# Local and global attention with two MLPs on one core: the last twelve steps' keys and queries copied through DRAM and transposed as fp32r

## The chip, the cores and the metric

The kernel runs on one core of a Trainium2 chip. The metric is the device time of one execution in microseconds (us). TensorE is written PE (its weight loads PEld), VectorE DVE, ScalarE ACT, GpSimd POOL; SyncE (SP) issues nearly all DMA transfers.

## What is computed

Attention comes first: 4 batches, 8 heads, 512 local and 32 global rows of 64 elements. Each local row looks at the global keys and at local keys at most 32 places away; each global row looks at all. Its output (2176 rows of 512) goes through two MLPs. The core of it:

```python
s_g = scale * q_g @ concat(k_g, k_l).T ; out_g = softmax(s_g) @ concat(v_g, v_l)
s_l = concat(scale * q_l @ k_g.T, where(|i - j| <= 32, scale * q_l @ k_l.T, -1e9))
out_l = softmax(s_l) @ concat(v_g, v_l)
x = concat(out_g, out_l)                      # 2176 x 512
h = x @ w_in    # 512 x 2048 ; x = maximum(0.01 * h, h) @ w_out
h = x @ w2_in ; out = (h - tanh(h)) @ w2_out
```

The weights arrive as 64-bit floats, the attention inputs as 32-bit floats.

## The kernel before

The attention is cut into 32 steps, `pp` = 0 to 31: a step is two heads of one half (256 rows) of one batch. Two neighbouring steps share one load group `g` = `pp // 2`, so there are 16 groups, and groups 10 to 15 (steps 20 to 31) are batch 2's second half and the whole of batch 3. `load_kq(g)` issues seven transfers on SP's queue: three key tiles `kr` and two pieces of global keys through `keyed`, and two query tiles `qr`; each has three buffers. `stage(s)` is the work of a step, and its `keys` part holds, in this order, `k_prep(s + 1)`, `q_prep(s + 1)` and, for even `s`, `load_kq((s + 6) // 2)`; so group 10 is loaded in stage 14 and first used in stage 19.

`k_prep` transposes a step's three key tiles on PE against the fp32 identity `ident` (128, 96 and 128 columns, into the PSUM bank `kps`), and ACT copies the bank out to `kt`. `q_prep` does the same with two tiles of 128 columns (`qps`, `qt`). `score` multiplies the two (`sps`), and softmax, the transposes of the probabilities (`p_trans`, `ptps`) and the product with the values (`av`, tile `vr`) follow.

The matmuls of the MLPs (`h`, `y`, and `o` in the second MLP) have fp32r operands: each fp32 operand is split into a high and a low fp32r part, and three products are added. The scores, the products with the values and all transposes are fp32.

A loop over `n` walks over 160 items. Items 0 to 79 are the first MLP, each one block `f` of 128 hidden columns for one piece of tokens `c`; the pieces are 512, 512, 256, 512 and 384 columns wide. Items 80 to 159 are the second MLP. The attention's steps 0 to 9 run ahead of the loop; the later ones are spread between the matmuls of the items by the table `beside`: steps 10 to 17 beside items 0 to 7, 18 to 21 beside items 24 to 31, 22 to 29 beside items 32 to 47, and the rest beside items 48 to 58. PE's order is the program's order (`manual_schedule`). The other engines and the DMA queues are put in order by a list scheduler that runs when the program is built: an instruction goes to its engine's queue when it is ready in a simulated timeline, and among ready ones the earlier in the program goes first. `tc.issue_after(x)` ties what its block issues behind the instruction `x`, in order only, and only what lies on the same engine as `x`.

Two such anchors matter here. `last_kq[0]` is the last query transfer issued so far (on SP from group 2 on), and `anchor[0]` is the last `tensor_sub` of `mlp1_g` (on DVE, line 215). Weights come by `load_w` (`inraw`, `wraw`) and go through DRAM (`wod`, `w2id`, `w2od`) as raw words.

Of the kernel before, what the change touches and what calls it, by code (L numbers as in the profile page):

```python
# [8 lines left out]
F32 = mybir.dt.float32  # L9
F32R = mybir.dt.float32r  # L10
# [11 lines left out]
def kernel(  # L22
# [14 lines left out]
    nc = tc.nc  # L37
    B, H, SL, D = q_l.shape
    SG = q_g.shape[2]
# [5 lines left out]
    HALF = SL // 2  # L45
# [13 lines left out]
    dram = ctx.enter_context(tc.tile_pool(name="dram", bufs=1, space=bass.MemoryType.DRAM))  # L59
    psum = ctx.enter_context(tc.tile_pool(name="psum", bufs=1, space=bass.MemoryType.PSUM))  # L60

    def bank(tag, name):
        return psum.tile([128, 512], F32, tag=tag, name=name)
# [15 lines left out]
    ident = persist.tile([128, 128], F32, name="ident")  # L79
# [15 lines left out]
    def f32(t):  # L95
        return t.bitcast(F32)
# [76 lines left out]
    anchor, anchor_s = [None], [None]  # L173
    last_av = [None]
    last_exp, last_min = [None], [None]
    last_kq, last_fetch = [None], [None]
# [109 lines left out]
    att = att_ctx.enter_context(tc.tile_pool(name="att", bufs=2))  # L286
# [6 lines left out]
    def build_masks():  # L293
        make_identity(nc, ident)
        nc.gpsimd.memset(mask, 0.0)
        make_identity(nc, ident_b)
        for a in range(2):
            for j in range(2):
                w0, w1 = windows[a][j]
                if w1 - w0 < WIN:  # L300
                    nc.gpsimd.memset(mask[:, a, j, w1 - w0 :], BIG)
                lo, hi = max(w0, SG), min(w1, KC - SG)
                k0 = first_key[a] + lo - SG - (a * HALF + j * 128)
                m = mask[:, a, j, lo - w0 : hi - w0]
                for base, step in ((32 - k0, -1), (32 + k0, 1)):
                    nc.gpsimd.affine_select(
                        out=m, in_=m, compare_op=ALU.is_ge, fill=BIG,
                        base=base, pattern=[[step, hi - lo]], channel_multiplier=-step,
                    )
# [20 lines left out]

    v_t = {}

    def place_of(g):
        hv, h0 = divmod(4 * g, H)
        b, a = divmod(hv, 2)
        return b, a, slice(h0, h0 + 4)

    def keyed(dst, local, glob, b, a, hs, queues=None):
        queues = queues or [nc.sync] * 3
        for t in range(3):  # L340
            k0 = first_key[a] + 96 * t
            l, g = (slice(32, 128), slice(0, 32)) if t == 0 else (slice(0, 96), slice(96, 128))
            queues[t].dma_start(out=dst[l, t], in_=local[b, hs, k0 : k0 + 96, :].rearrange("h s d -> s h d"))
            if t != 1:
                queues[t].dma_start(out=dst[g, t], in_=glob[b, hs].rearrange("h s d -> s h d"))

    def load_kq(g):

        if g >= NU // 4:
            return  # L350
        b, a, hs = place_of(g)
        qr = att.tile([128, 2, 4, D], F32, tag="qr", name="qr", bufs=3)
        kr = att.tile([128, 3, 4, D], F32, tag="kr", name="kr", bufs=3)

        keyed(kr, k_l, k_g, b, a, hs, [nc.sync, nc.sync, nc.scalar] if g == 0 else None)
        queue = nc.scalar if g < 2 else nc.sync
        for t in range(2):
            s0 = a * HALF + t * 128
            last_kq[0] = queue.dma_start(out=qr[:, t], in_=q_l[b, hs, s0 : s0 + 128, :].rearrange("h s d -> s h d"))
        for k in range(2):  # L360
            h2 = slice(2 * k, 2 * k + 2)
            raw_t[2 * g + k] = qr[:, :, h2, :], kr[:, :, h2, :]
# [12 lines left out]

    key_tiles = [(0, 128), (128, 96), (224, 128)]

    def k_prep(pp, tag):
        kr = raw_t[pp][1]
        ps = bank(tag, "kps")  # L380
        for t, (c, n) in enumerate(key_tiles):
            nc.tensor.transpose(ps[:, c : c + n], kr[:n, t].rearrange("p h d -> p (h d)"), ident[:n, :n])  # L382
        kt = att.tile([128, KC], F32, tag="kt", name="kt", bufs=2)
        nc.scalar.activation(kt, ps[:, :KC], AF.Copy)
        k_t[pp] = kt

    def q_prep(pp, tag):
        qr = raw_t[pp][0]
        ps = bank(tag, "qps")
        for t in range(2):  # L390
            nc.tensor.transpose(  # L391
                ps[:, t * 128 : t * 128 + 128], qr[:, t].rearrange("p h d -> p (h d)"), ident
            )
        qt = att.tile([128, HALF], F32, tag="qt", name="qt", bufs=2)
        nc.scalar.activation(qt, ps[:, :HALF], AF.Copy, scale=-0.125)
        q_t[pp] = qt
# [346 lines left out]
    def stores():  # L743
        while later:
            later.pop(0)()
# [38 lines left out]
    def in_job():  # L784
        *parts, high, low = in_parts() or [lambda: None] * 2
        for part in parts:
            behind(part)
        high()
        low()
# [170 lines left out]
    if True:  # L960
# [2 lines left out]
        nc.vector.memset(tc_a1, T_A1)  # L963
        nc.vector.memset(tc_a2, T_A2)
        build_masks()
        for e in e_t:
            nc.gpsimd.memset(e[:, :, :, 192:], 0.0)
        for t in (*qgd, vg):
# [8 lines left out]
        parts, lows = [], []  # L977
        for pp in range(PRE):
# [3 lines left out]
            if pp >= 2 and pp % 2 == 0:  # L982
                lows, parts = parts[5:], in_parts()
# [54 lines left out]
        for n in range(len(items) + 8):  # L1038
            ph, c, f = items[n] if n < len(items) else (3, 0, 0)
            one = items[n - 1] if 0 < n <= len(items) else (3, 0, 0)  # L1040
            if n in (2 * NF + 4, 3 * NF):
                tags[0] = run_tags + (["y2", "y3"] if n < 3 * NF else [])
            if ph == 1:
                if n in (0, 2, 4, 6) or HF <= n < 2 * HF:
                    in_job()
                if n in (0, 2) or 4 <= n < 12:
                    in_load()
                for _ in range(job_at.get(n, 0)):
                    job()
                if n in (3 * HF + 3, 3 * HF + 5):  # L1050
                    y_part((n - 3 * HF - 3) // 2)
                if c == 4 and f == 0:
                    while gtodo:
                        gtodo.pop(0)[1]()
                    assert not raws and not jobs
                    att_ctx.close()
                    p2 = ctx.enter_context(tc.tile_pool(name="p2", bufs=1))
                    for k in range(NF - 1):
                        wo2_t.append([p2.tile([128, ND, 128], F32R, name=f"wo2{x}{k}") for x in "hl"])
                    wo2_t.append([x[1][:, :, 512:] for x in (xh, xl)])  # L1060
                    x2_load(0, 0)
                    x2_load(0, 1)
                if c == 4:
                    w2_fetched = [fetch2(w2o_dram[f], False), fetch2(w2i_dram[f], f >= 2 + ND)]
                    if 2 <= f < 2 + ND:
                        x2_split(0, f - 2)
            elif ph == 2 and order2.index(c) + 1 < 5:
                nx = order2[order2.index(c) + 1]
                if f in (2, 3):
                    x2_load(nx, f - 2)  # L1070
                if 5 <= f < 5 + ND:
                    x2_split(nx, f - 5)
            if n in fetch_at:
                fetches.extend(items1[m][2] for m in fetch_at[n])
            while fetches:
                wo_fetch(fetches.pop(0))
            ops = beside.pop(n, [])
            if ph == 2:
                mlp2_a(c, f)
            if ph == 3:  # L1080
                while p_t:
                    mlp2_split()
            steps, last = [], []
            for k in b_at.get(n, []):
                p, c1, f1 = items[k]
                if p == 1:
                    steps += mlp1_b(c1, f1)
                else:
                    last.append((c1, f1))
            if ph == 1:  # L1090
                steps = mlp1_a(c, f) + steps
            if ph == 1 and not ops and gtodo:
                ops = [gtodo.pop(0)[1]]
            K, M = len(ops), len(steps)
            at = [int((i + 0.5) * M / K) for i in range(K)]
            for m, step in enumerate(steps):
                step()
                while at and at[0] <= m:
                    at.pop(0)
                    ops.pop(0)()  # L1100
            for op in ops:
                op()
            for c1, f1 in last:
                mlp2_b(c1, f1)
            if ph == 1 and c == 4:
                for kind, t in zip(("out", "in"), w2_fetched):
                    behind(lambda: w2_place(kind, f, t))
            fix(n + 1)
            stores()
# [30 lines left out]
```

## Time and profile before

| | us |
|---|---|
| median of 3 runs | 917.92 |
| lowest, highest | 917.36, 918.85 |
| the profiled execution | 918.29 |
| its span in the trace | 916.5 |
| PE busy in the span | 898.9 (98%) |
| DVE, ACT, POOL busy | 626.5, 537.5, 36.4 |

How to read it: the trace holds one execution, 1.8 us shorter in span than its own measured time. The page lists busy time by engine, then groups of instructions, with what ended the idle time before them. The view by stretches gives each engine's busy time, the granted PE clock and the DMA engines' busy share between two times. The timeline lists instructions with their start. A record of a matmul is longer than the time it holds PE, since neighbours overlap: its pace is read from the start of one to the start of the next.

### The profile page before, as it was taken

How to read it: one execution, taken by the hardware profiler on the slowest of the kernel's cores; microseconds unless marked ns; L12 is line 12 of the kernel's file. 1: busy time of each engine (PE TensorE's matmuls, PEld its weight loads, DVE VectorE, ACT ScalarE, POOL GpSimd, SP SyncE). 2: the span in 40 equal slices, each digit the busy share in tenths (PEclk: the TensorE clock that was granted, in tenths of full speed). 3: DMA queues.
4: the chain of work that ended last, by engine and by line, in shares of the span. 5: the costliest groups of instructions: out<-in, count | busy, mean ns of one | idle time of the engine just before them, and what ended most of it. 6: DMA issues, size and time to landing. Idle time of an engine off the chain costs nothing.

```text
span 916.5 us, 15297 instructions
## 1 busy us (share of the span) xinstructions
PE 898.9 (98%) x5384; PEld 759.6 (83%) x5384; DVE 626.5 (68%) x1374; ACT 537.5 (59%) x1245; POOL 36.4 (4%) x70
## 2 busy tenths in 40 slices
PE   7989999999999999999999999999999999999998
PEld 4667778888778999888889998888888888899897
DVE  3987876766546656552233459888878888888886
ACT  5988865444655676553243566565556555655564
POOL 4400000000000000000000000000000000000022
PEclk9999999999999999999999999999999999999999
DMA  8786796678767977756546762001000100010010
GB/s 194 213 207 194 225 313 219 204 237 255 241 183 232 277 212 235 266 191 186 193 167 205 249 196 81 0 18 65 1 1 24 46 1 1 1 46 1 1 36 24
DMA packets 133917, 129.20 MB, mean 141 GB/s; under 512 B 72400, under 2 KB 96208, under 8 KB 133840
## 3 DMA queue, kind: packets, MB, share of 16 engines
q1 hardware_dynamic: 131040, 127.44, 45.4%
q10 hardware_dynamic: 2800, 0.79, 0.4%
q8 instruction: 42, 0.69, 0.3%
q14 instruction: 35, 0.29, 0.1%
HBM read 101.45 MB, written 26.74 MB: 140 GB/s over the span
## 4 chain that ended last, share of the span: by engine, by line
PE 86%; ACT 4%; DMA 4%; DVE 4%; issue 1%; POOL 0%; SPq 0%; ACTq 0%; POOLq 0%; DVEq 0%
PE h L55 38%; PE o L55 20%; PE y L55 18%; DMA wraw<-in_moe_w_out_dram 2%; PE sps L55 2%; PE ptps L483 2%; PE avps L55 2%; ACT e L453 1%; PE kps L382 1%; PE sgps L55 1%; PE gavps L55 1%; PE qps L391 1%; DMA inraw<-in_moe_w_in_dram 1%; ACT g L213 1%; DVE wt L137 0%
## 5 line engine op out<-in xcount | busy, mean ns | idle before, releaser
L55 PE MATMUL h<-xh,win 128*128 128x512 f32 (+2 forms) x1280 | 355.1, 361 | 0.6 <-ACT g L213 0.6
L55 PEld LDWEIGHTS h<-xh,win 128*128 128x128 f32 x1280 | 229.3, 188 | 33.8 <-ACT g L213 1.8
L55 PE MATMUL h<-xl,win 128*128 128x512 f32 (+2 forms) x640 | 228.9, 358 | 0.0
L215 DVE TENSOR_TENSOR gl<-g,gh 128x512 fp32r<-128x512 f32 (+2 forms) x80 | 48.8, 610 | 133.8 <-ACT gh L214 133.7
L55 PEld LDWEIGHTS h<-xl,win 128*128 128x128 f32 x640 | 120.5, 188 | 15.3
L55 PE MATMUL y<-gh,woh 128*128 128x512 f32 (+2 forms) x320 | 119.2, 373 | 0.0
L55 PE MATMUL y<-gh,wol 128*128 128x512 f32 (+2 forms) x320 | 114.4, 357 | 0.0
L55 PE MATMUL y<-gl,woh 128*128 128x512 f32 (+2 forms) x320 | 114.1, 358 | 0.0
L213 ACT ACTIVATE g<-h 128x512 f32<-128x512 f32 (+2 forms) x80 | 42.6, 533 | 109.6 <-PE h L55 109.5
L55 PE MATMUL o<-wo2l,gh 128*128 128x512 f32 x255 | 99.6, 391 | 0.0
L55 PE MATMUL o<-wo2h,gh 128*128 128x512 f32 x255 | 99.4, 390 | 0.0
L55 PE MATMUL o<-wo2h,gl 128*128 128x512 f32 x255 | 97.4, 390 | 0.0
L667 ACT ACTIVATE u<-h 128x512 f32<-128x512 f32 (+2 forms) x80 | 42.6, 533 | 90.5 <-PE h L55 82.8
L692 ACT ACTIVATE gh<-p 128x512 fp32r<-128x512 f32 (+2 forms) x80 | 45.5, 568 | 41.0 <-DVE p L676 41.0
L55 PEld LDWEIGHTS y<-gh,woh 128*128 128x128 f32 x320 | 60.2, 188 | 8.8 <-issue 1.9
L55 PEld LDWEIGHTS y<-gl,woh 128*128 128x128 f32 x320 | 60.2, 188 | 7.9
L55 PEld LDWEIGHTS y<-gh,wol 128*128 128x128 f32 x320 | 60.3, 189 | 6.4
L453 ACT ACTIVATE e<-e,st 128x224 f32<-128x224 f32 (+1 forms) x88 | 40.3, 459 | 30.0 <-DVE st L446 29.8
L673 ACT ACTIVATE u<-u,consts 128x512 f32<-128x512 f32 (+2 forms) x80 | 52.7, 659 | 6.4 <-DVE p L671 3.8
L693 DVE TENSOR_TENSOR gl<-p,gh 128x512 fp32r<-128x512 f32 (+1 forms) x64 | 41.8, 653 | 21.4 <-ACT gh L692 21.3
L55 PEld LDWEIGHTS o<-wo2h,gl 128*128 128x128 f32 x255 | 47.8, 188 | 10.1
L55 PEld LDWEIGHTS o<-wo2l,gh 128*128 128x128 f32 x255 | 47.9, 188 | 9.0
(118 smaller groups left out, 1397.0 us busy)
## 6 DMA issues: line engine op xcount, KB each, us to landing
wraw<-in_moe_w_out_dram SPq DMA_DIRECT2D x32, 512.0 KB, 4.4
woh<-wod SPq DMA_DIRECT2D x64, 256.0 KB, 3.9
wol<-wod SPq DMA_DIRECT2D x64, 256.0 KB, 3.4
inraw<-in_moe_w_in_dram SPq DMA_DIRECT2D x16, 512.0 KB, 5.7
wraw<-in_moe_w_in_dram SPq DMA_DIRECT2D x16, 512.0 KB, 4.9
vr<-in_v_l_dram SPq DMA_DIRECT2D x48, 96.0 KB, 4.0
kr<-in_k_l_dram SPq DMA_DIRECT2D x47, 96.0 KB, 3.1
vn<-in_v_l_dram SPq DMA_DIRECT2D x8, 512.0 KB, 4.6
```

The lines of the kernel that those rows point to most:

```text
L55: nc.tensor.matmul(o, lhsT, rhs, start=start, stop=stop, skip_group_check=shared)
L213: nc.scalar.activation(g[:, :N], h[:, :N], AF.Prelu, alpha=0.01)
L215: anchor[0] = nc.vector.tensor_sub(gl[:, :N], g[:, :N], f32(gh)[:, :N])
L382: nc.tensor.transpose(ps[:, c : c + n], kr[:n, t].rearrange("p h d -> p (h d)"), ident[:n, :n])
L391: nc.tensor.transpose(ps[:, t * 128 : t * 128 + 128], qr[:, t].rearrange("p h d -> p (h d)"), ident)
L453: last_exp[0] = nc.scalar.activation(e[:, h, j, s0 : s0 + n], x, AF.Exp, bias=st[:, k : k + 1], scale=-1.0, accum_out=st[:, 4 + k : 5 + k],)
L483: nc.tensor.transpose(ps[:, at : at + n], e[:n, h, j, c0 : c0 + 128], ident[:n, :n])
L667: nc.scalar.activation(u, h, AF.Square)
L673: nc.scalar.activation(u, u, AF.Square, bias=tc_a2)
L692: nc.scalar.activation(gh[:, :N], p, AF.Copy)
L693: eng["pool" if i == order2[-1] else "dve"].tensor_sub(gl[:, :N], p, f32(gh)[:, :N])
```

## The change

For groups 10 to 15 keys and queries no longer come straight from the inputs. `stage_in` copies them unchanged from the inputs into DRAM tiles of the kernel (`k_st`, `q_st`, `kg_st`), and `load_kq` reads those tiles into `kr` and `qr`, which for these groups are declared fp32r and written through an fp32 view, so that the words stay as they are. Their transposes then take an fp32r identity, `ident_r`, which DVE copies from `ident` at the start. Batch 2's five copies stand at items 1 to 3 of the loop and carry `last_kq[0]` as anchor; batch 3's five stand at items 10, 12, 14, 16 and 18 and carry `anchor[0]`. A copy of keys or queries covers four heads; of batch 2 only rows from 224 (keys) and 256 (queries) on are copied.

```diff
+    G1 = 10
+    k_st, q_st = [dram.tile([2, H, SL, D], F32, name=f"{x}_st") for x in "kq"]
+    kg_st = dram.tile([2, H, SG, D], F32, name="kg_st")
+    ident_r = att.tile([128, 128], F32R, name="ident_r", bufs=1)
+    first_st = [SL - 288, 0], [HALF, 0]
+
+    def stage_in(b, part, anchor):
+        with tc.issue_after(anchor.ins):
+            if part == 0:
+                nc.sync.dma_start(out=kg_st[b - 2], in_=k_g[b])
+                return
+            dst, src, lo = ((k_st, k_l, first_st[0][b - 2]), (q_st, q_l, first_st[1][b - 2]))[part % 2]
+            hs = slice(0, 4) if part < 3 else slice(4, 8)
+            nc.sync.dma_start(out=dst[b - 2, hs, lo:], in_=src[b, hs, lo:])
...
-        qr = att.tile([128, 2, 4, D], F32, tag="qr", name="qr", bufs=3)
-        kr = att.tile([128, 3, 4, D], F32, tag="kr", name="kr", bufs=3)
-
-        keyed(kr, k_l, k_g, b, a, hs, [nc.sync, nc.sync, nc.scalar] if g == 0 else None)
+        dt = F32 if g < G1 else F32R
+        qr = att.tile([128, 2, 4, D], dt, tag="qr", name="qr", bufs=3)
+        kr = att.tile([128, 3, 4, D], dt, tag="kr", name="kr", bufs=3)
+
+        if g < G1:
+            q_in, bq = q_l, b
+            keyed(kr, k_l, k_g, b, a, hs, [nc.sync, nc.sync, nc.scalar] if g == 0 else None)
+        else:
+            q_in, bq = q_st, b - 2
+            keyed(f32(kr), k_st, kg_st, b - 2, a, hs)
...
+    def transposed(out, x, n):
+        if x.dtype == F32R:
+            nc.tensor.transpose(out.bitcast(F32R), x, ident_r[:n, :n])
+        else:
+            nc.tensor.transpose(out, x, ident[:n, :n])
...
-            nc.tensor.transpose(ps[:, c : c + n], kr[:n, t].rearrange("p h d -> p (h d)"), ident[:n, :n])
+            transposed(ps[:, c : c + n], kr[:n, t].rearrange("p h d -> p (h d)"), n)
...
         build_masks()
+        nc.vector.tensor_copy(ident_r, ident)
...
+            if 1 <= n < 4 or 10 <= n < 20 and n % 2 == 0:
+                b, parts = (2, (0, 1, 2, 3, 4)) if n < 4 else (3, (0, 1, 2, 3, 4))
+                for k in (parts[2 * n - 2 : 2 * n] if n < 4 else parts[(n - 10) // 2 :][:1]):
+                    stage_in(b, k, last_kq[0] if n < 4 else anchor[0])
```

## Rows read from the trace of the kernel before

**Rows 1.** The page's first lines: span, and each engine's busy time.
```profile
span 916.5 us, 15297 instructions
PE 898.9 (98%) x5384; PEld 759.6 (83%) x5384; DVE 626.5 (68%) x1374; ACT 537.5 (59%) x1245; POOL 36.4 (4%) x70
```

**Rows 2.** Busy time by stretches; the last three columns are PE clock, DMA share, GB/s.
```profile
core 0: us, PE busy (x) PEld busy (x) DVE busy (x) ACT busy (x) POOL busy (x), PEclk, DMA share, GB/s
36.00:60.00 24.00, 22.16 (x240) 16.89 (x241) 21.22 (x58) 21.75 (x75) 6.35 (x8) 1.00 0.85 228
60.00:77.00 17.00, 15.07 (x151) 11.10 (x148) 11.14 (x45) 15.10 (x49) 0.15 (x1) 1.00 0.80 209
77.00:90.00 13.00, 13.00 (x86) 10.31 (x86) 10.95 (x33) 9.72 (x26) 0.30 (x1) 1.00 0.67 198
...
226.00:375.00 149.00, 148.53 (x1222) 129.49 (x1221) 84.09 (x285) 93.17 (x273) 0.91 (x6) 1.00 0.78 234
```

**Rows 3.** Timeline of PE around the transposes of step 22: start, length, instruction.
```profile
266.18 0.62 PE L55 MATMUL h<-xh,win 128*128 128x512 f32 x2
...
266.87 0.47 PE L382 MATMUL kps<-ident,kr 128*128 128x128 f32 x3
267.18 0.38 PE L391 MATMUL qps<-ident,qr 128*128 128x128 f32 x2
267.31 0.71 PE L55 MATMUL h<-xh,win 128*128 128x512 f32 x2
```

**Rows 4.** The chain that ended last, in order of time: fp32r matmuls of three widths.
```profile
146.08 2.72 PE y L55 x12
...
503.43 2.08 PE y L55 x12
...
861.03 1.43 PE h L55 x12
```

**Rows 5.** Instructions of line 534, the transposes with 32 columns: min/median/max in ns.
```profile
L534 PE MATMUL qgps<-ident,qgr x16: 220/222/311, 6.6 to 297.4; 32*128 32x32 f32 x16
```

**Rows 6.** Timeline of PE: four such transposes in a row.
```profile
100.20 0.43 PE L534 MATMUL qgps<-ident,qgr 32*128 32x32 f32 x4
```

**Rows 7.** Timeline of ACT: the copies of the queries out of PSUM, steps 21 and 27.
```profile
254.40 0.38 ACT L395 ACTIVATE qt<-qps 128x256 f32<-128x256 f32 x1
...
328.49 0.38 ACT L395 ACTIVATE qt<-qps 128x256 f32<-128x256 f32 x1
```

**Rows 8.** Timeline of PE: the scores that read them, same two steps.
```profile
255.37 0.46 PE L55 MATMUL sps<-kt,qt 64*128 64x224 f32 x2
...
328.89 0.60 PE L55 MATMUL sps<-kt,qt 64*128 64x192 f32 x4
```

**Rows 9.** Timeline of SP's queue: transfers as they are issued, 26 to 95 us.
```profile
26.72 0.51 SPq L581 DMA_DIRECT2D vn<-in_v_l_dram  x1
...
30.53 0.38 SPq L343 DMA_DIRECT2D kr<-in_k_l_dram  x1
...
50.77 0.48 SPq L345 DMA_DIRECT2D vr<-in_v_g_dram  x1
...
74.33 1.51 SPq L359 DMA_DIRECT2D qr<-in_q_l_dram  x2
...
77.04 0.38 SPq L581 DMA_DIRECT2D vn<-in_v_l_dram  x1
82.43 0.35 SPq L113 DMA_DIRECT2D wraw<-in_moe_w_out_dram  x1
...
90.61 0.31 SPq L343 DMA_DIRECT2D kr<-in_k_l_dram  x1
```

**Rows 10.** Transfers into the value tile `vr` issued from 36 to 62 us.
```profile
DMA to landing us min/median/max: 2.6/5.3/6.9
```

**Rows 11.** Timeline of PE: the product with the values of step 8.
```profile
59.18 0.94 PE L55 MATMUL avps<-pt,vr 128*64 128x128 f32 x16
```

**Rows 12.** The page's traffic in 40 slices of the span, GB/s.
```profile
GB/s 194 213 207 194 225 313 219 204 237 255 241 183 232 277 212 235 266 191 186 193 167 205 249 196 81 0 18 65 1 1 24 46 1 1 1 46 1 1 36 24
```

More of the change, by code (lines that the diff above doesn't have):

```diff
@@ L358, in load_kq @@
             s0 = a * HALF + t * 128
-            last_kq[0] = queue.dma_start(out=qr[:, t], in_=q_l[b, hs, s0 : s0 + 128, :].rearrange("h s d -> s h d"))
+            last_kq[0] = queue.dma_start(
+                out=(qr if g < G1 else f32(qr))[:, t], in_=q_in[bq, hs, s0 : s0 + 128, :].rearrange("h s d -> s h d")
+            )
         for k in range(2):
@@ L390, in q_prep @@
         for t in range(2):
-            nc.tensor.transpose(
-                ps[:, t * 128 : t * 128 + 128], qr[:, t].rearrange("p h d -> p (h d)"), ident
-            )
+            transposed(ps[:, t * 128 : t * 128 + 128], qr[:, t].rearrange("p h d -> p (h d)"), 128)
         qt = att.tile([128, HALF], F32, tag="qt", name="qt", bufs=2)
```

## Prediction, made before the changed kernel ran

> **What bounds the kernel now.** I read the page's engine line first. PE is busy for 898.9 of 916.5 us [rows 1], so PE work taken away should shorten the run unless something else is just as late. That share is an average, so I then read the view by stretches. The changed steps lie between 226 and 375 us, where PE works 148.53 of 149 us and DVE and ACT have 56 to 65 us to spare: PE alone sets the pace there. From 36 to 60 us it is different: PE 22.16, DVE 21.22 and ACT 21.75 of 24 us are all nearly full, and the DMA engines are 0.85 busy. From 77 to 90 us the DMA share is 0.67 [rows 2]. So PE time is worth its full length late, and transfers are dangerous early. The granted clock is 1.00, the 2.4 GHz level, in every stretch read, and I expect it to stay.
>
> **What the transposes cost now.** A step has five: three into kps, two into qps. In step 22 kps starts at 266.87 and the next matmul at 267.31, 0.44 us later. That matmul's pair takes 0.71 us where the pair before the transposes took 0.62, so it is held 0.09 us more: together 0.53 us for five, some 108 ns for one of 128 columns and less for the one of 96 [rows 3]. The records themselves are longer, but they overlap, so only the steps between starts count.
>
> **What one costs as fp32r.** No row shows an fp32r transpose. The nearest rows are the fp32r matmuls at three widths: twelve take 2.72 us at 512 columns, 2.08 at 384 and 1.43 at 256, or 227, 173 and 119 ns each [rows 4]. The steps of 54 ns per 128 columns lie on one line, which gives 65 ns at 128 columns. Below that there is a floor: four fp32 transposes of only 32 columns occupy 0.43 us, and with 0.22 us for a record the step is (0.43 - 0.22) / 3 = 70 ns, although each still loads 128 columns of weights [rows 5, 6]. So the low end is 65 to 70 ns. The high end is today's 108, because words of 32 bits are moved either way. Dearer is possible too: nothing in the trace excludes that so narrow an fp32r operation takes a slower path. I take 68 ns, since the fp32r rows are the nearest in operand type: five take 0.34 us, and a step saves 0.53 - 0.34 = 0.19 us.
>
> One row beside it: a transpose's record here is 220 ns and more even with 32 columns [rows 5], most of it latency. The Trainium skill ("TensorE: Matmul & The Clock Gate", Part 4: PE-mode transpose) gives about 275 ns for a bf16 transpose inside a kernel and puts most of it down to the access latency of SBUF. Read as a price for each, it says that the type does not matter and the saving is zero; that is the first rival. The steps between starts in [rows 3] are far under 275 ns, so here the latency overlaps and the rule is not the pace.
>
> **What of it reaches the end.** Twelve steps change. The transposes feed ACT's copies, and those feed the scores, so ACT could become the later one. In step 27 the copy of the queries ends at 328.49 + 0.38 = 328.87 and the scores start at 328.89: ACT is already last there, and the saving is lost. In the other eleven steps there is room; the least is in step 21, where the copy ends at 254.78 and the scores start at 255.37, 0.59 us later [rows 7, 8]. So 11 x 0.19 = 2.1 us. After the loads nothing else of the step changes: five transposes, two ACT copies, the same widths.
>
> The copy of the identity runs once on DVE at the start, which by the program has only two memsets before it and no scores to read yet; I cost it at nothing, and it would cost its length, under 1 us, if DVE's first work waited behind it. The loads of groups 10 to 15 keep their number, rows and bytes, so SP's issue time for them stays.
>
> **What the copies cost.** Ten transfers are added. Batch 2's carry 2 x 294,912 (keys) + 2 x 262,144 (queries) + 65,536 bytes, 1.18 MB; batch 3's 4 x 524,288 + 65,536, 2.16 MB. All are issued on SP's queue, about 0.5 us of issue each, 5 us over the run. Batch 2's first two are tied behind group 8's last query, the other three behind group 9's, issued from 74.33 us. SP issues nothing between 77.42 and 82.43 us, and group 10 is loaded from 90.61 us on [rows 9]. At the 198 GB/s of that stretch [rows 2] 1.18 MB take 6 us, so they land before 90 us; if late, group 10's loads wait on SP and hold back what stands behind them: the next raw weights, the stores of `wod`, the `inraw` loads. Group 10 itself isn't needed before step 20, at about 240 us. Cost nothing, up to 1 us if the cover is gone.
>
> Batch 3's copies are the open point. Their anchor is a DVE instruction and they are issued on SP; the tie holds only on one engine, so it does not hold them. They have no inputs to wait for, so the scheduler may issue them at any point at which SP's simulated queue has nothing earlier ready. That it does so shows: the `vn` transfer at 26.72 us belongs to stage 6, and it is issued before group 5's keys of stage 4, at 30.53 us [rows 9]. The copies can therefore lie anywhere from about 27 us, where `vn` shows SP first out of earlier work, to the places that the program gives them, items 10 to 18. Hidden, they cost nothing; the third part prices the bad place. Their need, group 12's load at about 228 us, is far off in any case.
>
> **Sum.** 918.29 of the profiled execution less 2.1 is 916.2. That execution is 0.37 us above the median of 917.92, so against the median: 917.92 - 2.1 = 915.8 us.
>
> **Rival 1: the transposes hardly get shorter.** For it: a transpose moves full 32-bit words in both types, and today's 108 ns are about twice what 128 columns cost in the matmuls' line (54 ns), as if each word went in two halves. If that belongs to the word and not to the identity, nothing is saved: 917.9 us. If half the difference stays (about 88 ns), 11 x 0.1 = 1.1 us are saved: 916.8. Against it: the fp32r rows run at one column per step of 0.42 ns.
>
> **Rival 2: batch 3's copies are issued early and PE waits.** From 36 to 60 us the DMA engines have 0.15 x 24 = 3.6 us free [rows 2]. 2.16 MB at that stretch's 228 GB/s take 9.5 us, so what is queued behind slips by up to 5.9 us. The values of step 8 are issued until 50.77 us, land 5.3 us later in the median, at 56.1, and are used at 59.18 [rows 9 to 11]: 3.1 us of room. PE, in its fixed order, then waits 5.9 - 3.1 = 2.8 us. I allow the same once more for a second late load of that stretch, 5.6 us; with the 2.1 saved, 921.4 us. It decides as soon as the copies stand ahead of 50 us and cost more than 3.1 us of delay; after 60 us nothing is close enough.
>
> How they spread over the DMA engines adds to it. At the best slice's 313 GB/s [rows 12] one of the 16 engines moves 19.6 GB/s. The Trainium skill ("DMA: Bandwidth & Descriptors", "Why a DMA increments its semaphore by 16 and not by 1") says that a transfer runs on the largest number of engines, up to 16, that divides its outermost dimension on both sides: a copy whose outermost dimension is four heads gets four. By that rule one batch-3 copy puts 131 KB on each of four engines, an estimated 6.7 us, and the four copies 27 us, which would cost far more than 5.6 us in that stretch. No run here shows it; contiguous copies may be cut otherwise.
>
> **Rival 3: narrow fp32r is slower.** Four times the matmul line's column cost would be 4 x 54 = 216 ns a transpose: 12 x 5 x 0.108 = 6.5 us longer, 924.4 us. Only the lack of any fp32r row under 256 columns speaks for it.
>
> **How the numbers follow.** About 0.2% (1.84 us) is what a measurement of this kernel can tell from no change: under 916.08 counts as faster, over 919.76 as slower. Forecast, shorter transposes and hidden copies, 915.3 to 916.1 us: 0.36. Rival 1, 916.1 to 918.5: 0.34. Rival 2, 919.8 to 922 and above: 0.26. Rival 3: 0.04. So faster 0.36, same 0.34, slower 0.30. The low bound is the 65 ns of [rows 4] in all twelve steps, 12 x 0.205 = 2.5 us, and 0.5 us for the measurement: 914.9. The high bound takes in rival 2 at 922.5 and leaves its far end and rival 3 out.
>
> **What the profile will show.** Right: 60 PE transposes of lines for kps and qps with starts 65 to 70 ns apart, five in about 0.34 us; the h, y and o groups unchanged; PE's busy time down by about 2 us; batch 3's copies after 60 us. Rival 1: the same steps near 108 ns. Rival 2: those copies on SP ahead of 50 us, avps or gavps waiting for vr or vg, PE busy less than 22 of 24 us between 36 and 60 us. The forecast is also wrong if the new order on ACT and DVE, which the scheduler makes afresh, moves other waits by more than 1 us.

## Result and the profile after

| | before | after |
|---|---|---|
| median, us | 918.1 (917.36 to 918.85, 6 runs) | 924.26 (921.2 to 925.21, 6 runs) |
| the profiled execution | 918.29 | 923.55 |
| its span | 916.5 | 921.8 |
| PE busy in the span | 898.9 | 901.5 |

After takes 1.006 times as long as before, with a 95% interval of 1.0047 to 1.0073. By that ratio the change made the kernel 5.5 us slower (the medians lie 6.2 us apart); the forecast was 2.1 us faster. Rival 3 gave 924.4 us, within 0.2 us of the measured time, but by chance: it wanted slower fp32r transposes, and they got shorter, as the rows below show. Rival 2 gave 921.4 us, 3 us less than measured; its kind of loss is what happened.

The span grew by 5.3 us, PE's busy time by 2.6. So PE lost time in two ways, about half each: it stood idle 2.7 us longer, and it took longer over the same 5384 operations. The page's first lines of after, which answer to [rows 1]:

```profile
span 921.8 us, 15307 instructions
PE 901.5 (98%) x5384; PEld 761.8 (83%) x5384; DVE 627.7 (68%) x1375; ACT 537.3 (58%) x1245; POOL 36.1 (4%) x70
```

PE runs its operations in one fixed order in both kernels, so the start of the same operation can be compared, and the difference tells at each point how late after is. At 66.7 us of before it is 0.08 us late, at 72 us 3.51, at 130 us still 3.52, at 142 us 6.30, at 222 us 6.39, at 380 us 5.46, and it stays there. So in this execution the loss falls in two short places, and the steps with the new transposes (226 to 375 us) give back 0.93 us.

The first place, in the timeline of PE in before (start, length, instruction, and in brackets the idle time ahead of it with what ended it):

```profile
66.68 0.44 PE L55 MATMUL sgps<-kt,qgd 128*64 128x128 f32 x4
67.87 0.31 PE L55 MATMUL gavps<-pg,vg 96*64 96x32 f32 x4 [0.75 <-DVE st L446]
68.01 0.64 PE L55 MATMUL gavps<-pg,vn 128*64 128x32 f32 x16
```

and in after:

```profile
66.76 0.44 PE L55 MATMUL sgps<-kt,qgd 128*64 128x128 f32 x4
70.21 0.31 PE L55 MATMUL gavps<-pg,vg 96*64 96x32 f32 x4 [3.02 <-DMA vg<-in_v_g_dram]
70.32 0.95 PE L55 MATMUL gavps<-pg,vn 128*64 128x32 f32 x16
71.20 1.22 PE L55 MATMUL h<-xh,win 128*128 128x512 f32 x2
72.22 0.63 PE L55 MATMUL h<-xl,win 128*128 128x512 f32 x1
```

What ends the wait has changed: in before it is DVE, after 0.75 us; in after it is the load of `vg`, after 3.02 us. PE is then 70.21 - 67.87 = 2.34 us late, of which 0.08 were there already. Then the work behind it is slower: a wide matmul's record is 0.63 us where it is 0.39 elsewhere. The view by stretches of after tells why (columns as in [rows 2]):

```profile
36.00:60.00 24.00, 22.26 (x238) 16.92 (x238) 21.29 (x58) 21.74 (x74) 6.28 (x8) 1.00 0.86 258
60.00:77.00 17.00, 13.71 (x110) 10.18 (x106) 8.89 (x33) 11.58 (x37) 0.15 (x1) 0.90 0.84 219
70.20:74.00 3.80, 3.79 (x29) 3.25 (x30) 1.40 (x5) 0.51 (x2) 0.00 (x0) 0.55 0.87 187
134.00:160.00 26.00, 23.82 (x132) 19.25 (x131) 13.99 (x26) 11.96 (x24) 0.00 (x0) 0.93 0.78 253
```

From 70.2 to 74 us the granted clock is 0.55, so nearly all of it is the 1.2 GHz level, right behind the 3 us of idle PE. In before it is 1.00 there [rows 2]. In all, 3.51 - 2.34 = 1.2 us more are lost up to 72 us. The second place is the same load of a later stage. Before, then after:

```profile
133.93 0.31 PE L55 MATMUL gavps<-pg,vg 96*64 96x32 f32 x4 [0.93 <-DMA vg<-in_v_g_dram]
138.70 0.39 PE L55 MATMUL gavps<-pg,vg 96*64 96x32 f32 x4 [2.18 <-DMA vg<-in_v_g_dram]
```

Before waits 0.93 us for that load; after waits 2.18, so 1.25 more, and the clock takes another 1.5 us (4.78 us late at 133.9 of before, 6.30 at 142).

Now why `vg` is late at the first place. SP's queue in after, 36 to 66 us, which answers to [rows 9]:

```profile
35.92 0.99 SPq L113 DMA_DIRECT2D wraw<-in_moe_w_out_dram  x2
36.95 0.61 SPq L344 DMA_DIRECT2D kg_st<-in_k_g_dram  x1
37.61 0.58 SPq L348 DMA_DIRECT2D q_st<-in_q_l_dram  x1
38.23 0.65 SPq L348 DMA_DIRECT2D k_st<-in_k_l_dram  x1
39.01 0.51 SPq L360 DMA_DIRECT2D vr<-in_v_l_dram  x1
...
48.45 1.44 SPq L554 DMA_DIRECT2D qgr<-in_q_g_dram  x1
49.93 0.51 SPq L348 DMA_DIRECT2D q_st<-in_q_l_dram  x1
50.48 0.59 SPq L348 DMA_DIRECT2D k_st<-in_k_l_dram  x1
51.16 0.53 SPq L360 DMA_DIRECT2D vr<-in_v_l_dram  x1
...
54.48 0.52 SPq L362 DMA_DIRECT2D vr<-in_v_g_dram  x1
...
65.72 1.10 SPq L613 DMA_DIRECT2D vg<-in_v_g_dram  x1
```

These are all five of batch 3's copies. The program gives them at its items 10 to 18; they are issued at 37 and 50 us, over 180 us before group 12 is loaded, and ahead of `vr` and `vg`. SP issues one transfer behind the other here, and the five take 0.61 + 0.58 + 0.65 + 0.51 + 0.59 = 2.9 us of it. Everything behind them moves: the last `vr` of step 8 from 50.77 us [rows 9] to 54.48, and `vg` from 60.19 us in before,

```profile
60.19 1.40 SPq L584 DMA_DIRECT2D vg<-in_v_g_dram  x1
```

to 65.72, 5.5 us. The five issues are 2.9 of these; the rest are issues and waits of SP behind them that grew longer, as the first `inraw` at 60.16 us with 1.90 us (0.51 before). PE needed `vg` at 67.87. Batch 2's five copies are issued where the program gives them, from 70.65 us on.

The transposes of step 22 in after, beside [rows 3]:

```profile
273.14 0.38 PE L405 MATMUL kps<-ident_r,kr 128*128 128x128 f32 x3
273.36 0.34 PE L405 MATMUL qps<-ident_r,qr 128*128 128x128 f32 x2
273.53 0.69 PE L55 MATMUL h<-xh,win 128*128 128x512 f32 x2
```

By the prediction's own reading: 273.53 - 273.14 = 0.39 us, and the next pair is held 0.69 - 0.62 = 0.07 us. Five take 0.46 us; they took 0.53, and 0.34 was forecast.

### The profile page after: what moved, and what is told of

The parts are those of the page before. It is cut to its first block, busy times and chain, and to the rows that moved or that the text cites. A ratio compares the mean times of both kernels' runs of the same rounds, so it can differ in the third digit from the quotient of the medians.

```text
span 921.8 us, 15307 instructions
## 1 busy us (share of the span) xinstructions
PE 901.5 (98%) x5384; PEld 761.8 (83%) x5384; DVE 627.7 (68%) x1375; ACT 537.3 (58%) x1245; POOL 36.1 (4%) x70
## 4 chain that ended last, share of the span: by engine, by line
PE 87%; DMA 4%; ACT 4%; DVE 3%; issue 1%; SPq 1%; POOL 0%; ACTq 0%; DVEq 0%; POOLq 0%
PE h L55 39%; PE o L55 20%; PE y L55 18%; PE sps L55 2%; DMA wraw<-in_moe_w_out_dram 2%; PE ptps L512 2%; PE avps L55 2%; ACT e L482 1%; PE gavps L55 1%; DMA vg<-in_v_g_dram 1%; PE sgps L55 1%; DMA vr<-in_v_l_dram 1%; DVE st L469 1%; DVE wt L137 0%; ACT g L213 0%
## 5 line engine op out<-in xcount | busy, mean ns | idle before, releaser
L55 PEld LDWEIGHTS o<-wo2h,gh 128*128 128x128 f32 x255 | 48.0, 188 | 9.0
```

Of the source, the lines that this page charges most:

```text
L55: nc.tensor.matmul(o, lhsT, rhs, start=start, stop=stop, skip_group_check=shared)
```

## Experiments

Three questions stand: do batch 3's copies cause the whole loss, is it SP's issue time or the bytes, and what paces an fp32r transpose?

**Late copies.** Batch 3's copies are tied behind a transfer of SP's own queue, where the tie holds:

```
-  stage_in(b, k, last_kq[0] if n < 4 else anchor[0])
+  stage_in(b, k, last_kq[0] if n < 4 else last_fetch[0])
```

> Edit: batch 3's five copies carry the last fetch of the weights (a transfer on SP) as anchor instead of a DVE instruction, so they are issued between 145 and 200 us; all else as in the changed kernel. Theory A (the early copies of batch 3 delay the loads of vg, PE waits near 70 us and its clock falls; those of batch 2 cause the second stretch of loss near 139 us; the transposes save about 1.1 us): the 3.9 us lost near 70 us are gone, the 2.7 us near 139 us stay, 918.1 + 2.7 - 1.1 = 919.7 us. Rival B (both losses come from batch 3): 917.0 us. Rival C (the new order of the other engines loses the time, wherever the copies lie): 924 us.

Measured: 917.39 us beside 918.21, ratio 0.9992 (0.998 to 1.0003). The copies are now issued from 157.65 to 180.58 us, among the stage's other transfers. By the medians rival B holds: with these five transfers moved, the loss is gone.

The profiled execution is the slowest of its ten, 921.75 us. In it PE is nearly on time at the first place (0.2 us late at 72 us), but 3.2 us late at 142 us. The profile of the same kernel's repetition below (922.59 us) shows the same, 4.9 us late at 142 us. Waits of PE in the two (us in total, times, longest), where before has 0.9:

```profile
PE gavps L55 <- DMA vg<-in_v_g_dram: 2.4, 1, 2.4
PE gavps L55 <- DMA vg<-in_v_g_dram: 2.8, 1, 2.8
```

Batch 3's copies come only after that wait in both. So the loss at the second place also comes without early copies, in some executions; what makes `vg` late there is open, and that the early copies cause it in after is not shown. What they are shown to cost is the loss at the first place; how the rest of the median's loss divides is open.

**Only batch 3 staged, early.** Batch 2 is loaded as before:

```
-  G1 = 10
+  G1 = 12
...
-  if 1 <= n < 4 or 10 <= n < 20 and n % 2 == 0:
+  if 10 <= n < 20 and n % 2 == 0:
```

> Edit: batch 2 is not staged (its groups 10 and 11 load and transpose as before), batch 3's copies lie as in the changed kernel. Theory A: the loss near 70 us stays, 3.9 us, the one near 139 us goes, and eight steps save 0.7 us: 921.3 us. Rival B (both losses from batch 3): 918.1 + 6.6 - 0.7 = 924.0 us. Rival D (both from batch 2): 917.4 us.

Measured: 922.3 us, 1.0043 (1.0028 to 1.0058), between the two theories. In its profiled execution PE is 3.1 us late by 60 us and 4.9 by 72 us, with no copy but batch 3's. At the second place nothing is lost: it is 3.9 us late at 142 us.

**fp32 instead of fp32r.** All copies as in after, but the tiles and transposes of the last twelve steps stay fp32:

```
-  dt = F32 if g < G1 else F32R
+  dt = F32
```

> Edit: all copies and loads as in the changed kernel, but the tiles of groups 10 to 15 are fp32 again, and so are their transposes. It prices the copies alone. Theory A: the losses near 70 and 139 us stay, and the 1.1 us that the transposes save are gone: 924.3 + 1.1 = 925.4 us. If the fp32r transposes cost time elsewhere (a slower neighbour, a later score), it is at or under 924.3 us.

Measured: 924.38 us, 1.0064 (1.0039 to 1.009). The loss is there without any fp32r transpose, so rival 3 of the prediction is out. Here a `vr` is late as well as `vg`, for which PE waits 1.69 us at 71.89; timeline of PE:

```profile
47.87 1.67 PE L55 MATMUL avps<-pt,vr 128*64 128x128 f32 x16 [1.72 <-DMA vr<-in_v_g_dram]
```

[rows 11] show sixteen of these in 0.94 us; here they take 1.67, at the lower clock. Which loads are waited for changes from execution to execution: in the first profile of after `vg` alone, in a second one both, as here (5.8 us late at 72 us).

**Only batch 2 staged.** Its five copies and four fp32r steps:

```
-  dt = F32 if g < G1 else F32R
+  dt = F32R if g in (10, 11) else F32
...
-  if 1 <= n < 4 or 10 <= n < 20 and n % 2 == 0:
+  if 1 <= n < 4:
```

> Edit: only batch 2 is staged and transposed as fp32r (groups 10 and 11, four steps); batch 3 loads and transposes as before. Theory A: no loss near 70 us, 2.7 us near 139 us, four steps save 0.35 us: 920.4 us. Rival B (both losses from batch 3): 917.7 us.

Measured: 917.94 us, 1.0001 (0.9989 to 1.0014). So no cost of batch 2's copies shows, as the prediction had it; the interval leaves room for more than 1 us.

**Five tiny copies.** The kernel with late copies, and at the five early places copies of 4 KB, whose data is not used:

```
+  tiny_st = dram.tile([5, 16, D], F32, name="tiny_st")
...
-  stage_in(b, k, last_kq[0] if n < 4 else anchor[0])
+  stage_in(b, k, last_kq[0] if n < 4 else last_fetch[0])
+  if b == 3:
+      nc.sync.dma_start(out=tiny_st[k], in_=k_l[3, 0, 16 * k : 16 * k + 16])
```

> The kernel with batch 3's copies tied late (917.4 us), and at the five early places on SP's queue (behind the raw weights at 37 us, and at 50 us) five copies of 4 KB each into a DRAM tile that nothing reads. Theory I (SP's issue time: five issues of about 0.6 us in a queue that runs back to back): vr and vg are issued 2 to 3 us later as in the changed kernel, PE waits 1 to 3 us for one of them before 75 us and loses 1.5 us more at the 1.2 GHz clock: 920 to 921.5 us. Theory B (the 2.16 MB occupy the DMA engines): nothing is lost, 917.4 us. If it is both, between: 918.5 to 920.

Measured: 921.3 us beside 919.38 on that chip, 1.0021 (1.0005 to 1.0037). It costs something without the bytes, but less than after: neither theory alone. The profiled execution does not show where: it is on time at 72 us (0.06 us late) and loses 3.2 us at the second place, as the late copies without the tiny ones did.

**Copies from GpSimd's queue.** Batch 3's copies are issued on GpSimd, tied behind its work of steps 6 and 9 (`pool_at` keeps those instructions):

```
-  nc.sync.dma_start(out=dst[b - 2, hs, lo:], in_=src[b, hs, lo:])
+  (nc.sync if b == 2 else nc.gpsimd).dma_start(out=dst[b - 2, hs, lo:], in_=src[b, hs, lo:])
...
-  stage_in(b, k, last_kq[0] if n < 4 else anchor[0])
+  stage_in(b, k, last_kq[0] if n < 4 else pool_at[6 if k < 3 else 9])
```

> The changed kernel with batch 3's five copies issued from GpSimd's queue, tied behind its work of steps 6 and 9, so that they start at about 42 and 50 us and cost SP no issue time. Theory I (SP's issue time): no wait, 917.5 us, with at most 0.5 us for the issues on GpSimd. Theory B (bytes): vr or vg land 3 us or more later, PE waits before 75 us and the clock falls: 921.5 to 924 us.

Measured: 924.82 us beside 919.38, 1.0052 (1.0034 to 1.0071). Taking the issues off SP brings nothing back. But it is no clean test: in the profiled execution, which was the fastest of its ten (920.4 us), the issues stand between GpSimd's multiplies of `e`, and PE also waits there (us in total, times, longest):

```profile
PE ptps L512 <- POOL e L496: 0.8, 2, 0.5
```

**Smaller pieces.** Each copy of keys or queries is cut into 16 rows at the outside:

```
-  nc.sync.dma_start(out=dst[b - 2, hs, lo:], in_=src[b, hs, lo:])
+  nc.sync.dma_start(
+      out=dst[b - 2, hs, lo:].rearrange("h (a s) d -> a h (s d)", a=16),
+      in_=src[b, hs, lo:].rearrange("h (a s) d -> a h (s d)", a=16),
+  )
```

> The changed kernel with each copy of keys and queries cut into 16 rows at the outside, in pieces of 4.6 to 8 KB a head, issued at the same places. Theory I (SP's issue time) and theory B (bytes) both leave the loss: 923 to 925 us. Theory P (the pieces of 32 KB, 1.2 to 1.4 us each, hold an engine while the small rows of vr and vg stand behind them): the small pieces take turns with the loads and the wait goes: 917.5 to 920 us.

Measured: 924.29 us beside 919.38, 1.0047 (1.0028 to 1.0065). Theory P falls. The trace of after holds the four uncut copies of batch 3 as 64 packets of 32,768 bytes, so each was in sixteen pieces already; the cut makes the pieces smaller. The time from issue to landing of the 512 KB copies is not shorter either (transfers, KB each, median us):

```profile
q_st<-in_q_l_dram SPq DMA_DIRECT2D x2, 512.0 KB, 6.9
k_st<-in_k_l_dram SPq DMA_DIRECT2D x2, 512.0 KB, 7.3
```

Uncut, in the kernel with only batch 3 staged:

```profile
q_st<-in_q_l_dram SPq DMA_DIRECT2D x2, 512.0 KB, 6.1
k_st<-in_k_l_dram SPq DMA_DIRECT2D x2, 512.0 KB, 7.2
```

**The four on one chip.** After, the late copies and the tiny copies once more, with the edits above, and a fourth with only batch 3 staged and its copies late (the first two edits together), so that the loss can be divided.

> The changed kernel itself, beside the next three on one chip, so that its loss can be divided: before + 5.5 us, as in its first comparison (1.006).

> The changed kernel with batch 3's copies tied behind a transfer of SP's own queue. Both theories of the loss (issue time, bytes) take it away: 11 steps x 0.09 us of the shorter transposes are left as a gain, before - 1.0 us (0.999). If the late copies cost something too, it is before or slower.

> The kernel with late copies and five copies of 4 KB at the early places; their data is not used. What it is slower than the kernel with late copies is the price of five issues alone; what the changed kernel is slower than this one is the price of 2.16 MB at those places. Theory I (issue time alone): as the changed kernel, before + 5.5 us. Theory B (bytes alone): as the late copies, before - 1.0. From its first look I expect both: 2.7 us for the issues, before + 1.7, and the rest for the bytes.

> Only batch 3 is staged, its copies tied late, and eight steps have the fp32r transposes. If batch 2's copies are free, eight of twelve steps are saved: before - 0.7 us. If they cost something (they stand at 70 to 85 us, where vr loads are queued behind them), this one is faster than the kernel with all late copies: before - 1.5 us or more.

| kernel | median, us | ratio to before (918.15), 95% interval |
|---|---|---|
| after | 924.38 | 1.0055 (1.0037 to 1.0073) |
| late copies | 917.85 | 0.9996 (0.9985 to 1.0007) |
| late copies, five tiny early | 919.44 | 1.0014 (1.0004 to 1.0025) |
| only batch 3 staged, late | 917.19 | 0.9987 (0.9978 to 0.9996) |

Five issues alone cost (1.0014 - 0.9996) x 918.15 = 1.7 us; the 2.16 MB cost (1.0055 - 1.0014) x 918.15 = 3.8 us more. Both theories were half right, and the bytes seem the larger part. The intervals leave the first an uncertainty of more than 1 us and the second of nearly 2.

In the profile of the tiny copies `vg` is issued at 64.67 us, with next to no bytes added; in that of the late copies, its fair measure, at 62.17. So the five issues moved it by 2.5 us. The other profiles bear this out: with no early copies `vg` is issued at 59.97 to 62.17 us, with early tiny ones at 62.63 and 64.67, with the bytes alone (GpSimd's queue) at 63.71, with both (uncut) at 65.72 to 67.06. With the tiny copies PE is 1.4 us late by 60 us and 3.5 by 72; the lower clock stands there too (0.57 from 70.2 to 74 us):

```profile
70.20:74.00 3.80, 3.80 (x29) 3.25 (x30) 2.09 (x8) 1.61 (x5) 0.00 (x0) 0.57 0.78 181
```

The fourth kernel is the only one whose interval lies wholly below 1: 0.0013 x 918.15 = 1.2 us under before. It is the version to keep. In its profile no stretch up to 160 us has lost anything; PE's stretch of the second place is again

```profile
134.00:160.00 26.00, 26.00 (x148) 21.41 (x149) 18.89 (x34) 13.35 (x25) 0.00 (x0) 1.00 0.70 233
```

as in before. Between 200 and 222 us this profile loses 0.9 us; the one with only batch 2 staged, which has no copy of batch 3, loses 0.6 there, and why is open. Against the one with all late copies the intervals overlap, so that batch 2's copies cost something is not shown. The loss at the second place came only in profiles of kernels with batch 2's copies, but not in all of them.

**Transposes back to back.** A kernel of its own, which computes nothing of the reference:

```
for kind in ("f", "r"):
    for name, n, m in [("a", 128, 128), ("b", 96, 128), ("c", 32, 128), ("d", 128, 64)]:
        for k in range(32):   # x[:n, c : c + m] against ident[:n, :n]
            nc.tensor.transpose(...)
```

> A kernel of its own that computes nothing of the reference: 32 transposes back to back of each of four shapes (rows x columns of the data: 128 x 128, 96 x 128, 32 x 128, 128 x 64), first fp32, then fp32r, and 24 fp32r matmuls of 512, 256 and 128 columns. Theory W (the pace of an fp32r transpose is its weight load, which goes by the data's columns): 128 x 128, 96 x 128 and 32 x 128 all at 80 to 90 ns, 128 x 64 at about half; the matmul of 128 columns at 80 to 90 too. Theory M (the matmul's columns set it, 54 ns for 128 and a floor of 65 to 70): 128 x 128 at 65 to 70 ns, fewer rows no more than that. In fp32 both expect 105 to 110 ns for 128 x 128, and W expects 32 x 128 nearly as long, M far less.

Timeline of PE (some of the fp32 operations ran earlier, while PE waited for its data):

```profile
28.04 1.14 PE L84 MATMUL faps<-ident,x 128*128 128x128 f32 x9
29.02 2.56 PE L84 MATMUL fbps<-ident,x 96*128 96x96 f32 x29
31.51 2.17 PE L84 MATMUL fcps<-ident,x 32*128 32x32 f32 x32
33.61 3.69 PE L84 MATMUL fdps<-ident,x 128*64 128x128 f32 x32
37.05 4.82 PE L87 MATMUL warm<-xr 128*128 128x512 f32 x20
41.71 2.88 PE L82 MATMUL raps<-ident_r,xr 128*128 128x128 f32 x32
44.42 2.86 PE L82 MATMUL rbps<-ident_r,xr 96*128 96x96 f32 x32
47.21 2.85 PE L82 MATMUL rcps<-ident_r,xr 32*128 32x32 f32 x32
49.99 2.24 PE L82 MATMUL rdps<-ident_r,xr 128*64 128x128 f32 x22
```

The pace is the time from the start of a group to the next, divided by its count. fp32: 0.98 / 9 = 109 ns for 128 rows, 2.49 / 29 = 86 for 96, 2.10 / 32 = 66 for 32 rows, and 3.44 / 32 = 108 for 128 rows with half the columns. So it goes by the data's rows, which are the identity's columns. fp32r: 2.71 / 32 = 85, then 87 and 87 ns for 128, 96 and 32 rows: the rows make no difference. With 64 columns the first ones stand 58 to 64 ns apart (after a first step of 84), so here the data's columns count, and these are the columns that the weight load reads. The fp32r transposes are as theory W had them. Two of its other expectations failed: fp32 with 32 rows takes 66 ns, far less than 108, and fp32r matmuls of 128 columns, expected at 80 to 90, take 2.60 / 24 = 108 (view by stretches: PE, weight loads, DVE, GpSimd, clock):

```profile
66.40:69.00 2.60, 2.60 (x26) 2.60 (x24) 0.00 (x0) 0.00 (x0) 1.00 0.00 0
```

That the weight load is what sets the 85 ns is thus likely from the columns, but not shown. The Trainium skill ("TensorE: Matmul & The Clock Gate", "LDWEIGHTS (loading the stationary operand)") says that a weight load takes as long for 32 rows as for 128, since its columns set it; the three equal fp32r rows agree. Its formula, columns divided by 1.2, gives an estimate of 107 ns for 128 columns, above the 85 measured.

## Why the prediction was wrong, step by step

**What bounds it.** Right in both halves: the transposes' saving late reached the end (6.39 us late at 222 us, 5.42 at 450 and from there on), and transfers were dangerous early.

**Batch 3's copies (the step that failed).** The prediction saw that their tie does not hold, that they "can therefore lie anywhere from about 27 us", and that they are costly ahead of 50 us. Then it took them as hidden and gave the bad place 0.26. They stand exactly there, at 37 and 50 us, and moved late they cost nothing that shows (0.9992 and 0.9996). Its own row should have decided: [rows 9] show SP issue a transfer of stage 6 ahead of one of stage 4, that is, take what has no inputs to wait for as soon as it can. No row spoke for the late place.

**The size of rival 2.** It had 2.16 MB delaying what is behind by up to 5.9 us, 3.1 us of room, 2.8 us of waiting, and the same once more. Measured in the profiled execution: `vg` issued 5.5 us later, 2.3 us of waiting, and 1.25 us more at a second load. The stretch was wrong: "after 60 us nothing is close enough", but both waits come after it, and PE's 22.26 of 24 us from 36 to 60 us are not the sign that rival 2 named. Two terms were missing. The clock: "I expect it to stay" at 1.00, but each of these two waits was followed by a stretch at 1.2 GHz that cost 1.2 to 1.5 us, 2.7 us together. With the smaller saving this is why 921.4 fell short: 918.29 + 3.55 of waits + 2.7 - 0.97 = 923.6. The Trainium skill ("TensorE: Matmul & The Clock Gate", "HAM oscillation — how this bites in real kernels") describes a matmul loop that waits for data and comes back at the lower clock; the rows of after agree in that, for single waits. In before the same `vg` waits were 0.75 us (for DVE) and 0.93 us, and the clock is 1.00 behind them, so [rows 2] did not hold this case. And the issue time: 5 us over the run were named and charged nowhere. The five early ones alone are 2.9 us in a full queue, which delays every load behind them, and cost about 1.7 us at the end.

The rule about engines (the Trainium skill, "DMA: Bandwidth & Descriptors", "Why a DMA increments its semaphore by 16 and not by 1") was weighed there too, with an estimated 6.7 us for a copy of four heads on four engines. The copies do take 6.1 to 7.2 us to land, but not for that reason: they moved as sixteen packets each, not four, as the prediction allowed for contiguous copies. So no run here tests the four engines.

**Batch 2's copies.** Right as far as the runs tell: 1.0001 (0.9989 to 1.0014).

**The transposes (a mis-sized term).** A step was to save 0.19 us, eleven steps 2.1. How late the kernels are at 222 us and at 450 us tells the saving by itself, since nothing is lost between: after 6.39 and 5.42, 0.97 us for twelve steps; only batch 3 staged, late, 0.89 and 0.31, 0.58 us for eight; only batch 2 0.26 us for four, by the same difference; with fp32 tiles 5.52 and 5.54, nothing. That is 0.07 to 0.08 us a step, less than half of the forecast. The pace of 68 ns was taken from the matmuls' line in [rows 4] and from the floor in [rows 5, 6]. The floor came from fp32 transposes with 32 rows and was carried over to fp32r; the transposes back to back show that rows shorten only the fp32 ones, and that fp32r stays at 85 to 87 whatever the rows. The matmuls' line does not reach down to 128 columns either: it gave 65 ns there, and the matmuls took 108. So the 96-row transpose of a step gains nothing (86 against 87), and the other four 109 - 85 = 24 ns each: 0.096 us, of which 0.08 show. Rival 1's half-way case (88 ns, 1.1 us) came out, by luck: its reason was words in two halves, and the rows speak for the columns. Whether ACT swallows the saving of step 27 cannot be told from 0.97 us.

**The identity's copy.** Right: at 30 us PE is 0.06 us late.

**The rest of the sum.** For the profiled execution: 916.5 us of span, 2.3 + 1.2 for the first place, 1.25 + 1.5 for the second, less 0.97: 921.8, the span of after.

## What to carry to other kernels

A tie behind an instruction of another engine does not hold a transfer that waits for nothing: find its place in the queue before pricing it, and tie it behind a transfer of its own queue. Where an issuing queue runs back to back, price each added transfer by its issue time as well as its bytes, and follow the delay to the load with the least room. Price a new wait of PE with the slower matmuls that may follow it, and take the pace of an operation from rows of its own type.

## What the runs showed of the hardware

A wait of 3.02 us on PE was followed by a granted clock of 0.55 over the next 3.8 us, and a wait of 2.18 us by one of 0.93 over 26 us; the price was 1.2 to 1.5 us each. Behind the 2.8 us wait in the second profile of the late copies the clock was 0.50 from 138 to 142 us, and the price was 2.9 us. Not every such wait was followed by it: with the copies on GpSimd's queue a wait of 1.55 us at the second place was not (clock 1.00, columns as in [rows 2]), though one of 1.72 us was with fp32 tiles.

```profile
134.00:160.00 26.00, 24.45 (x141) 19.83 (x140) 17.30 (x31) 13.14 (x24) 0.00 (x0) 1.00 0.78 253
```

In the kernel of transposes alone the clock fell although PE was never idle. View by stretches (PE, weight loads, DVE, GpSimd, then the clock):

```profile
47.30:49.90 2.60, 2.60 (x32) 2.60 (x32) 0.26 (x1) 0.00 (x0) 1.00 0.00 0
50.00:50.50 0.50, 0.50 (x9) 0.50 (x9) 0.19 (x1) 0.00 (x0) 0.93 0.00 0
50.50:53.00 2.50, 2.50 (x27) 2.50 (x25) 0.00 (x0) 0.00 (x0) 0.50 0.04 7
```

PE had done nothing but fp32r transposes since 41.71 us when it went to the 1.2 GHz level. Through 9 us of fp32 transposes (28 to 37 us) the clock had stayed at 1.00. In after, five transposes at a time among matmuls did not lower it (1.00 from 230 to 400 us).
